# Retention and soft mixture of experts on one core: input rows without gaps, one product moved ahead of a wait, the first expert layer by column halves, one weight load more in flight

## The chip, the cores and the metric

The kernel runs on one core of a Trainium2 chip. The metric is the device time of one execution in microseconds (us), as the median of the runs shown; 0.3% of it is about 0.48 us.

## What is computed

A retention layer (4 batches, 8 heads, 768 steps, head size 64) gives 3072 tokens of 512 values. A soft mixture of 8 experts with 4 slots each follows. All is float32.

```python
state = gamma * state + k_t (outer) v_t          # per batch and head, t = 0..767
y_t   = scale * q_t @ state
x = y as [3072, 512]
logits = x @ phi                                 # phi [512, 32 slots]
d = softmax of logits over the tokens;  slot_input = d.T @ x        # [8 experts, 4, 512]
for e in range(8):
    slot_out[e] = maximum(slot_input[e] @ w1[e], 0) @ w2[e]          # w1 [512, 1024], w2 [1024, 512]
out = (softmax of logits over the slots) @ slot_out                  # [3072, 512]
```

## The kernel before

**Stages.** The sequence is cut into 24 steps of 128 tokens (6 chunks of 4 batches). Two steps make one pass `P` of the loop (12 passes). A pass computes scores (`score_mm`, masked on DVE by `score_mask`), the values under the scores (`attend_mm`), the part from the running state (`carry_mm`, state tile `sall`), the state's update, the turned result (`natural_mm`), and for every four steps the logits and the dispatch of tokens to slots. After the loop comes the dispatch of the last group, whose result is the slot inputs `siT`.

**Experts.** `hidden(g, k)` multiplies slot inputs by first-layer weights. `g` is one of two groups of four experts, `k` one of four pieces of the contraction. All 32 slots are the stationary side; the four experts of a group stand in four column strips of TensorE (`tile_position=(0, 32*j)`), and each of the two halves of the 1024 hidden columns has a PSUM bank of its own. So group 0 ends before group 1 begins, and each group fills two banks. `hidden_t(g)` turns the result, eight 128x128 transposes for each group, and eight small DVE operations for each group take the four slots of each expert out of it (with the ReLU) into `hT`. The second layer runs in three column blocks (`BLOCKS`: 256, 128, 128 wide). `finish` spreads a block to the tokens and stores it; there are eight stores.

**Order.** The order on every engine is the order of the code (`manual_schedule`). All transfers go through one queue, SP's, in the order of the code, and a transfer is issued when its buffer is free and when the transfer eight places before it has landed (eight landing semaphores in turn). Input tiles have 6 buffers (`inp`), weights 13 (`big`), and a ring of 9 half-size tiles (`ring`) serves the rest. Weights are 32 loads of 1 MB: 16 for the first layer, 16 for the second. They are loaded while the loop runs, as many per pass as `PACE` says; in the last pass the freed input buffers and four ring slots take further ones (`load_halves(2)`, `load_weights(2)`), so that 21 loads are issued by then. The other 11 wait until `hidden` has freed a buffer.

**Inputs.** A step's input row holds keys, queries, values and keys again in the other layout, 2048 values for each of 128 partitions. Ten of the 23 rows are loaded without the last quarter (`TURNED` and the last four steps): 1536 of 2048 values, so that 6 KB are read and 2 KB skipped on each partition. The first step has a tensor of its own.

**The beginning** is written out ahead of the loop: score 0, its mask, a turn, the values of heads under score 0 in two parts, with the scores of step 1 between them.

Of the kernel before, what the change touches and what calls it, by code (L numbers as in the profile page):

```python
# [23 lines left out]
NSLOT = 32  # L24
# [19 lines left out]
NRING = 9  # L44
PACE = (1, 1, 1, 2, 1, 2, 1, 2, 2, 0, 2, 2)
TURNED = (0, 1, 2, 3, 4, 8, 12)

K_MASK, K_VSC, K_YT = 0, 128, 176
K_ID, K_QT, K_GC, K_J, K_ALL = 272, 400, 496, 500, 504
# [32 lines left out]
def retention_soft_moe_kernel(  # L82
    ctx: ExitStack,
    tc: tile.TileContext,
    in_: bass.AP,
    phi: bass.AP,
    w1: bass.AP,
    w2: bass.AP,
# [34 lines left out]
    nmc = small("nmc", [128, 2])  # L123
    zrun = zc[:, 0:1]
    wsel = small("wsel", [128, NSLOT])
    siT = small("siT", [128, NK, NSLOT])
# [18 lines left out]


    w1t, w2t, w2n = {}, {}, [0]
    weights = [("w1", 4 * g + 2 * jj, k) for g in range(2) for k in range(NK) for jj in range(2)]
    for cb, (_, w) in enumerate(BLOCKS):
        weights += [("w2", e, cb) for e in range(0, NE, 256 // w)]  # L150

    def load_weights(n):
        for _ in range(n):
            if not weights:
                return
            which, e, k = weights.pop(0)
            t = large(weight_pool[0])
            if which == "w1":
                nc.sync.dma_start(t, w1[e // 2, k])
                w1t[e, k], w1t[e + 1, k] = t[:, 0:FF], t[:, FF:2 * FF]  # L160
            else:
                nc.sync.dma_start(t, w2[w2n[0]])
                w2n[0] += 1
                w = BLOCKS[k][1]
                for j in range(256 // w):
                    for fc in range(NFC):
                        w2t[e + j, k, fc] = t[:, (j * NFC + fc) * w:(j * NFC + fc + 1) * w]

    def load_halves(n):
        for _ in range(n):  # L170
            _, e, k = weights.pop(0)
            assert k == 0
            for h in range(2):
                t = slot()
                nc.sync.dma_start(t, w2[w2n[0], :, h * 1024:(h + 1) * 1024])
                for fc in range(4):
                    w2t[e, k, 4 * h + fc] = t[:, fc * 256:(fc + 1) * 256]
            w2n[0] += 1

    st = {}  # L180
# [2 lines left out]
    def load_in(i):  # L183
        t = large(inp)
        st[i] = dict(kT=t[:, 0:512].rearrange("p (g t) -> p g t", t=C),
                     qT=t[:, 512:1024].rearrange("p (g t) -> p g t", t=C),
                     v=t[:, 1024:1536].rearrange("p (h e) -> p h e", e=D),
                     kn=t[:, 1536:2048].rearrange("p (h d) -> p h d", d=D))
        if i == 0:
            nc.sync.dma_start(t[:, 0:1024], first_[0])  # L190
            nc.sync.dma_start(first, first_[1])
            st[i]["v"] = first[:, K_ALL:K_ALL + 512].rearrange("p (h e) -> p h e", e=D)
        elif i in TURNED or i >= NSTEP - B:
            nc.sync.dma_start(t[:, 0:1536], in_[i - 1, :, 0:1536])
        else:
            nc.sync.dma_start(t, in_[i - 1])

    def turn_k(i, name, ident=ident):
        kp = bank(name)
# [231 lines left out]
    carry_mm(0)  # L431
    turn_k(0, "S", first[:, K_ID:K_ID + 128])
    warm(1)
    attend_mm(0, [0], (0, 1))
    score_mm(1)
    attend_mm(0, [0], (2, 3))
    score_mask(1)
    decay_table(ytab, K_YT)
    turn_k(1, "sm")
    for P in range(NPP):  # L440
# [40 lines left out]
            load_weights(2)  # L481
        attend_mm(P)
        if last:
            break
        attend_copy(P)
        if P < NPP - B // 2:
# [27 lines left out]
            combine_a(g - 1)  # L514

    weight_pool[0] = big
    dispatch_z(g - 1)
    dispatch_acc(g - 1)
    attend_copy(NPP - 1)
# [34 lines left out]
    nc.vector.tensor_scalar(zi, zp, 1e-9, None, ALU.add)  # L554
    nc.vector.reciprocal(zi, zi)
    warm(1, "A0")
    nc.vector.tensor_tensor(siT, sp, zi.unsqueeze(1).broadcast_to([128, NK, NSLOT]), ALU.mult)
    turn_l(g)
    combine_c(g - 1)
    combine_a(g)  # L560

    hs = {}
    hp = {}

    def hidden(g, k):
        if k == 0:
            hp[g] = [bank(n) for n in (("A2", "Y1"), ("Y0", "S"))[g]]
        for hf in range(2):
            for j in range(4):
                nc.tensor.matmul(hp[g][hf][32 * j:32 * j + 32, :], siT[:, k, :],  # L570
                                 w1t[4 * g + j, k][:, hf * 512:(hf + 1) * 512],
                                 start=(k == 0), stop=(k == NK - 1), skip_group_check=True,
                                 tile_position=(0, 32 * j))
        if k == NK - 1:
            hs[g] = slot()
            nc.scalar.copy(hs[g][:, 0:512], hp[g][0])
            nc.vector.tensor_copy(hs[g][:, 512:1024], hp[g][1])

    def hidden_t(g):
        for hf in range(2):  # L580
            tp = bank(("A2", "Y1")[hf]).rearrange("p (f t) -> p f t", t=128)
            for f in range(4):
                fc = hf * 4 + f
                nc.tensor.transpose(tp[:, f, :], hs[g][:, fc * 128:(fc + 1) * 128], ident)
            for j in range(4):
                a = 36 * j + 16 * g
                e = 4 * g + j
                nc.vector.tensor_scalar(hT[hf][:, :, e, 4 * e:4 * e + 4], tp[:, :, a:a + 4], 0.0, None, ALU.max)

    for k in range(NK):  # L590
        hidden(0, k)
        load_weights(2)
        if k == 0:
            hT = [slot().rearrange("p (f e s) -> p f e s", e=NE, s=NSLOT) for _ in range(2)]
            for t in hT:
                nc.vector.memset(t, 0.0)
            combine_b(NGRP - 1)
            combine_c(NGRP - 1)
    hidden(1, 0)
    load_weights(2)  # L600
    hidden(1, 1)
    hidden_t(0)
    load_weights(2)
    hidden(1, 2)
    load_weights(2)
    hidden(1, 3)
    load_weights(len(weights))


    co_tags = ["sm", "A2", "Y1", "A3", "S"]  # L610
    pend = []
# [31 lines left out]

    for cb, (c0, w) in enumerate(BLOCKS):
        op = bank(("A0", "A1")[cb % 2])
        for g in range(2):
            for fc in range(NFC):
                for j in range(4):
                    nc.tensor.matmul(op[32 * j:32 * j + 32, :w], hT[fc // 4][:, fc % 4, 4 * g + j, :],  # L649
                                     w2t[4 * g + j, cb, fc],  # L650
                                     start=(g == 0 and fc == 0), stop=(g == 1 and fc == NFC - 1),
                                     skip_group_check=True, tile_position=(0, 32 * j))
                if cb == 0 and g == 0 and fc == 2:
                    hidden_t(1)
                for f in pend:
                    next(f, None)
# [10 lines left out]
def lay_out(q, k, v, moe_phi, moe_w1, moe_w2):  # L667
    f = np.float32

    def tr(x):  # L670
        x = np.asarray(x).reshape(B, NPAIR, 2, NC, C, D)
        return x.transpose(3, 0, 2, 5, 1, 4).reshape(NSTEP, 128, 512)

    def nat(x):
        x = np.asarray(x).reshape(B, H, NC, C, D)
        return x.transpose(2, 0, 3, 1, 4).reshape(NSTEP, C, 512)


    heads = np.concatenate([head_of(np.arange(2), g) for g in range(NPAIR)])
    phi = np.asarray(moe_phi).reshape(H, D, NSLOT)[heads].reshape(NPAIR, 128, NSLOT).transpose(1, 0, 2)  # L680
    w1 = np.asarray(moe_w1).reshape(NE, H, D, FF)[:, heads].reshape(NE // 2, 2, NK, 128, FF).transpose(0, 2, 3, 1, 4)
    w2 = []
    for c0, w in BLOCKS:
        x = np.asarray(moe_w2)[:, :, c0:c0 + w].reshape(NE * w // 256, 256 // w, NFC, 128, w)
        w2.append(x.transpose(0, 3, 1, 2, 4).reshape(-1, 128, 2 * FF))
    kt, qt, vn = tr(k), tr(q), nat(v)
    return dict(x=np.concatenate([kt, qt, vn, nat(k)], axis=2)[1:], phi=phi,
                w1=w1.reshape(NE // 2, NK, 128, 2 * FF), w2=np.concatenate(w2),
                first=np.stack([np.concatenate([kt[0], qt[0]], axis=1),
                                np.concatenate([constants(), vn[0], np.zeros((128, 1024 - K_ALL - 512), f)], axis=1)]))  # L690

# [20 lines left out]
```

## Time and profile before

| what | value |
|---|---|
| median of 3 runs | 160.35 us (160.19 to 160.71) |
| the profiled execution's own time | 159.53 us |
| its span, first to last instruction | 157.8 us |
| PE busy | 147.1 us (93%) |
| DVE / ACT / POOL busy | 81.5 / 39.8 / 57.7 us |
| data moved by SP's queue | 62.46 MB, 96.8% of 16 engines over the span |

Sums below are made on the profiled execution, which is 0.82 us under the median. A busy share tells how full an engine was, not whether the end waited for it: here PE and the transfer queue are both nearly full, so the rows have to tell which of the two the last store waits for. The transfers of one load are split over 16 transfer engines, and a load has landed when the last of them is done.

### The profile page before, as it was taken

The page shows a single profiled execution, that of the slowest core. Times are in us where ns is not written, and L with a number is a line of the kernel's source. Part 1 is how long each engine was busy: PE and PEld are TensorE (multiplying, and loading weights), DVE is VectorE, ACT ScalarE, POOL GpSimd, SP SyncE. Part 2 cuts the span into 40 slices and gives each one's busy share as a digit, 9 for nine tenths or more (in the row PEclk, how much of TensorE's full clock was granted, in tenths as well). Part 3 has the DMA queues.
Part 4 walks back from the last instruction along what each step waited for, and adds up shares of the span by engine and source line. Part 5 has one row for each costly group of instructions (what it writes and reads, how often), then busy time and mean ns, then how long its engine had stood idle before and what let it go on. Part 6 is the DMA issues. An engine that isn't in the chain of part 4 may idle for free.

```text
span 157.8 us, 5512 instructions
## 1 busy us (share of the span) xinstructions
PE 147.1 (93%) x2418; PEld 108.3 (69%) x2418; DVE 81.5 (52%) x203; ACT 39.8 (25%) x95; POOL 57.7 (37%) x63
## 2 busy tenths in 40 slices
PE   8979999999999999999998989999999999999720
PEld 2569989997999789978996867864324565666400
DVE  0349607573847484758573856578312302555320
ACT  3311551315052305040504031330010100534220
POOL 0343696975737486384738365010100000000000
PEclk9999999999999999999999999999999999999975
DMA  5899999999999999999999999999999999999993
GB/s 205 301 348 422 426 422 415 415 424 413 414 419 418 418 420 420 415 418 420 409 415 423 409 423 415 408 410 397 370 426 422 426 418 424 409 409 416 420 402 125
DMA packets 9816, 62.81 MB, mean 398 GB/s; under 512 B 1088, under 2 KB 1216, under 8 KB 4288
## 3 DMA queue, kind: packets, MB, share of 16 engines
q1 hardware_dynamic: 9792, 62.46, 96.8%
q8 instruction: 19, 0.31, 0.8%
q14 instruction: 5, 0.04, 0.1%
HBM read 56.16 MB, written 6.29 MB: 396 GB/s over the span
## 4 chain that ended last, share of the span: by engine, by line
PE 85%; DMA 4%; DVE 3%; ACT 1%; issue 1%; SPq 1%; ACTq 0%; DVEq 0%
PE A L222 14%; PE Y L255 13%; PE A L649 9%; PE A L299 8%; PE S L283 6%; PE Y L246 6%; DMA b<-in_x_dram 4%; PE Y L570 4%; PE sm L316 4%; PE S L374 3%; PE A L570 2%; PE S L570 2%; PE A L633 2%; DVE r L230 2%; PE A L201 1%; PE sm L633 1%
## 5 line engine op out<-in xcount | busy, mean ns | idle before, releaser
L230 DVE TENSOR_TENSOR r<-A,kt 128x512 f32<-128x512 f32 x46 | 28.7, 682 | 18.3 <-PE A L222 18.3
L207 POOL TENSOR_TENSOR b<-b,qtab 128x512 f32<-128x512 f32 x20 | 25.5, 1280 | 24.0 <-DMA b<-in_x_dram 18.9
L222 PE MATMUL A<-b 64*128 64x128 f32 x384 | 25.2, 279 | 0.9 <-DMA b<-in_x_dram 0.9
L212 POOL TENSOR_TENSOR b<-b,kt 128x512 f32<-128x512 f32 x23 | 23.7, 1049 | 4.7 <-DMA b<-in_x_dram 4.7
L222 PEld LDWEIGHTS A<-b 64*128 64x128 f32 x384 | 22.5, 187 | 4.1 <-issue 2.6
L255 PE MATMUL Y<-r,b 128*64 128x128 f32 x352 | 22.5, 276 | 0.2
L255 PEld LDWEIGHTS Y<-r,b 128*64 128x64 f32 x352 | 19.1, 137 | 2.8 <-issue 2.3
L649 PE MATMUL A<-b,r 128*32 128x128 f32 (+1 forms) x352 | 15.9, 304 | 0.0
L649 PEld LDWEIGHTS A<-b,r 128*32 128x32 f32 x352 | 10.6, 110 | 7.1 <-issue 4.4
L306 ACT COPY r<-A 128x512 f32<-128x512 f32 x23 | 12.4, 591 | 9.9 <-PE A L299 9.9
L299 PE MATMUL A<-kt,r 128*128 128x128 f32 x96 | 13.3, 279 | 0.4 <-ACT r L274 0.4
L299 PEld LDWEIGHTS A<-kt,r 128*128 128x128 f32 x96 | 10.4, 140 | 1.7 <-ACT r L274 0.7
L283 PE MATMUL S<-b 128*64 128x64 f32 x304 | 11.0, 222 | 0.4 <-issue 0.4
L283 PEld LDWEIGHTS S<-b 128*64 128x64 f32 x304 | 10.5, 138 | 0.5 <-issue 0.5
L246 PE MATMUL Y<-b,sst 64*64 64x128 f32 x304 | 10.7, 276 | 0.0
L406 POOL TENSOR_TENSOR cn<-cn,cz 128x128 f32<-128x128 f32 x6 | 2.4, 401 | 19.9 <-DVE cz L405 15.5
L275 DVE COPY r<-Y 128x512 f32<-128x512 f32 x9 | 6.2, 691 | 6.2 <-PE Y L255 6.2
L246 PEld LDWEIGHTS Y<-b,sst 64*64 64x64 f32 x304 | 8.3, 132 | 1.2
L316 PEld LDWEIGHTS sm<-r,phis 128*32 128x32 f32 x192 | 6.2, 110 | 3.3 <-issue 3.3
L633 PE MATMUL A<-cT,r 32*128 32x384 f32 x26 | 8.3, 529 | 0.0
L570 PE MATMUL Y<-b,siT 128*32 128x512 f32 x64 | 8.2, 594 | 0.0
L316 PE MATMUL sm<-r,phis 128*32 128x128 f32 x192 | 7.4, 273 | 0.0
(139 smaller groups left out, 176.4 us busy)
## 6 DMA issues: line engine op xcount, KB each, us to landing
b<-in_w_dram SPq DMA_DIRECT2D x30, 1024.0 KB, 14.8
b<-in_x_dram SPq DMA_DIRECT2D x13, 1024.0 KB, 12.2
b<-in_x_dram SPq DMA_DIRECT2D x10, 768.0 KB, 11.9
out_dram<-b SPq DMA_DIRECT2D x8, 768.0 KB, 8.2
r<-in_w_dram SPq DMA_DIRECT2D x4, 512.0 KB, 11.9
b<-in_first_dram SPq DMA_DIRECT2D x1, 512.0 KB, 3.3
r<-in_first_dram SPq DMA_DIRECT2D x1, 512.0 KB, 4.1
phis<-in_phi_dram SPq DMA_DIRECT2D x1, 64.0 KB, 10.3
```

The source lines that it names most:

```text
L207: nc.gpsimd.tensor_tensor(q, q, qtab, ALU.mult)
L212: nc.gpsimd.tensor_tensor(v, v, vsc[:, i // B, a:b].unsqueeze(2).broadcast_to([128, b - a, D]), ALU.mult)
L222: nc.tensor.matmul(s["sc"][r][:, g, :], s["kT"][half(r), g, :], s["qT"][half(r), g, :], start=True, stop=True, skip_group_check=True)
L230: nc.vector.tensor_tensor(s["A"][:, r, g:g + n], s["sc"][r][:, g:g + n], mask.unsqueeze(1).broadcast_to([128, n, C]), ALU.mult)
L246: nc.tensor.matmul(p["y"][k][b][half(half_of(r, g)), gl, :], sst[(2 * P + k) % B][half(r), g, :], s["qT"][half(r), g, :], start=(gl == 0 a ...
L255: nc.tensor.matmul(pr[P]["y"][k][g // 2][half(half_of(r, g)), g % 2, :], s["v"][:, 2 * g + r, :], s["A"][:, r, g, :], start=(P < B // 2 an ...
L283: nc.tensor.matmul(S_[half(r), k, g, :], s["kn"][:, 2 * g + r, :], s["v"][:, 2 * g + r, :], start=True, stop=True, skip_group_check=True)
L299: nc.tensor.transpose(X[k][:, g * 128:(g + 1) * 128], pr[P]["yT"][:, k, g, :], ident)
L316: nc.tensor.matmul(q["ltp"][32 * j:32 * j + 32, :], phis[:, p, :], st[GRP * g + j]["yT"][:, p, :], start=(p == 0), stop=(p == NPAIR - 1), ...
L570: nc.tensor.matmul(hp[g][hf][32 * j:32 * j + 32, :], siT[:, k, :], w1t[4 * g + j, k][:, hf * 512:(hf + 1) * 512], start=(k == 0), stop=(k ...
L633: nc.tensor.matmul(cp, s4[32 * j:32 * j + 32, m * 128:(m + 1) * 128], cT[32 * j:32 * j + 32, 3 * h:3 * h + 3, :], start=True, stop=True, s ...
L649: nc.tensor.matmul(op[32 * j:32 * j + 32, :w], hT[fc // 4][:, fc % 4, 4 * g + j, :], w2t[4 * g + j, cb, fc], start=(g == 0 and fc == 0), s ...
```

## The change

1. **Rows without gaps.** The ten short rows get a tensor of their own (`in3`, 1536 values per partition, one behind the other), the thirteen whole ones another (`in4`). Size and number of loads stay.
2. **First values.** `attend_mm(0, [0])` does all heads ahead of `score_mm(1)`.
3. **First layer by column halves.** `hidden(hf, g, k)`: both groups of a half accumulate into one bank. For this `siT` is widened (it now lies in `qtab`, which is free by then) and padded with zeros, so that a window of 32 columns that starts 4*j further on holds one expert's slots in rows 0 to 3 (group 0) or 16 to 19 (group 1), and zeros in the other group's rows. One half takes four transposes and two DVE operations. A `w1` load holds one half of four experts, and the order of the `w2` loads of the first block, and of its products, follows the halves.
4. **A 22nd load.** `load_halves(1, sall)` in the last pass loads one more pair of second-layer halves, one into the state tile (no longer read) and one into a ring slot.
5. The zeroing of `hT` goes from DVE to GpSimd (POOL), where the new zeroing of the widened `siT` stands too.

```diff
-            nc.sync.dma_start(t[:, 0:1536], in_[i - 1, :, 0:1536])
+        elif i in LEAN:
+            nc.sync.dma_start(t[:, 0:1536], in3[LEAN.index(i)])
...
-    attend_mm(0, [0], (0, 1))
+    attend_mm(0, [0])
     score_mm(1)
-    attend_mm(0, [0], (2, 3))
...
         attend_mm(P)
         if last:
+            load_halves(1, sall)
             break
...
+    hp = [bank(n) for n in ("A2", "Y0")]
+    hs = slot()
+    def hidden(hf, g, k):
+        for j in range(4):
+            a = g * NK * SIW + k * SIW + 4 * j
+            nc.tensor.matmul(hp[hf][32 * j:32 * j + 32, :], si0[:, a:a + NSLOT],
+                             w1t[hf, g, k][:, j * 512:(j + 1) * 512],
+                             start=(g == 0 and k == 0), stop=(g == 1 and k == NK - 1), skip_group_check=True,
+                             tile_position=(0, 32 * j))
+        if g == 1 and k == NK - 1:
+            h = hs[:, hf * 512:(hf + 1) * 512]
+            nc.scalar.copy(h[:, 0:256], hp[hf][:, 0:256])
+            nc.vector.tensor_copy(h[:, 256:512], hp[hf][:, 256:512])
...
+    for hf in range(2):
+        for g2 in range(2):
+            for k in range(NK):
+                hidden(hf, g2, k)
+                load_weights(1)
...
+                        nc.gpsimd.memset(t, 0.0)
...
+                if (hf, g2, k) == (1, 0, 0):
+                    hidden_t(0)
```

PE at the beginning, before (L222 scores, L255 values under the scores, L201 turn of keys; `A` and `Y` are PSUM banks, `r` and `b` tiles):

```order
L255 MATMUL Y_123<-r 64x128 x4
L222 MATMUL A_137<-b 128x128
L222 MATMUL A_138<-b 128x128
...
L255 MATMUL Y_124<-r 64x128 x4
L201 MATMUL sm<-kt,b 128x128 x4
L222 MATMUL A_169<-b 128x128
```

The same place after (L264 values, L231 scores, L210 turn):

```order
L264 MATMUL Y_122<-r 64x128 x4
L264 MATMUL Y_123<-r 64x128 x4
L231 MATMUL A_140<-b 128x128
L231 MATMUL A_141<-b 128x128
...
L210 MATMUL sm<-kt,b 128x128 x4
L231 MATMUL A_168<-b 128x128
```

The second four products have moved ahead of the eight scores of step 1, which wait for its input.

SP's queue around the last pass, before (`b` and `r` are weight tiles and ring slots):

```order
L159 DMA b<-in_w_dram 128x2048 x3
L162 DMA b<-in_w_dram 128x2048
L175 DMA r<-in_w_dram 128x1024 x4
L162 DMA b<-in_w_dram 128x2048 x13
L639 DMA out_dram<-b 128x1536 x8
```

The same place after (`sst` is the state tile):

```order
L167 DMA b<-in_w_dram 128x2048 x3
L170 DMA b<-in_w_dram 128x2048
L185 DMA r<-in_w_dram 128x1024 x4
L170 DMA b<-in_w_dram 128x2048 x2
L185 DMA sst<-in_w_dram 128x1024
L185 DMA r<-in_w_dram 128x1024
L170 DMA b<-in_w_dram 128x2048 x10
L648 DMA out_dram<-b 128x1536 x8
```

Of the 13 loads before the stores, one has become two halves that stand ahead of the ten which wait for `hidden`.

PE in the first expert layer, the last part before (L570 first layer, L584 transposes, L649 second layer):

```order
L570 MATMUL Y_1756<-b,siT 32x512 x4
L570 MATMUL S<-b,siT 32x512 x4
L584 MATMUL A_1778<-kt,r 128x128 x4
L584 MATMUL Y_1787<-kt,r 128x128 x4
L570 MATMUL Y_1756<-b,siT 32x512 x4
```

The whole layer after, up to the second transposes (L584 first layer, L597 transposes, L659 second layer):

```order
L584 MATMUL A_1696<-b,qtab 32x512 x32
L584 MATMUL Y_1697<-b,qtab 32x512 x4
L597 MATMUL Y_1765<-kt,r 128x128 x4
L584 MATMUL Y_1697<-b,qtab 32x512 x28
...
L597 MATMUL S<-kt,r 128x128 x4
```

The 64 products are the same in number and shape; sixteen transposes have become eight, and one bank is written 32 times in a row.

## Rows read from the trace of the kernel before

**Rows 1.** Page, parts 2 and 3: transfers in 40 slices; instruction fetches (packets, MB, share).

```profile
DMA  5899999999999999999999999999999999999993
GB/s 205 301 348 422 426 422 415 415 424 413 414 419 418 418 420 420 415 418 420 409 415 423 409 423 415 408 410 397 370 426 422 426 418 424 409 409 416 420 402 125
...
q8 instruction: 19, 0.31, 0.8%
```

**Rows 2.** SP's timeline, narrow windows: start and length in us of one issue each.

```profile
150.04 0.33 SPq L639 DMA_DIRECT2D out_dram<-b  x1
151.48 0.33 SPq L639 DMA_DIRECT2D out_dram<-b  x1
...
101.67 0.33 SPq L162 DMA_DIRECT2D b<-in_w_dram  x1
109.81 0.33 SPq L162 DMA_DIRECT2D b<-in_w_dram  x1
```

**Rows 3.** Issues in narrow windows: KB, us to landing (0.8, 150, 151.5, 101.7, 109.8).

```profile
b<-in_first_dram SPq DMA_DIRECT2D x1, 512.0 KB, 3.3
...
out_dram<-b SPq DMA_DIRECT2D x1, 768.0 KB, 4.8
...
out_dram<-b SPq DMA_DIRECT2D x1, 768.0 KB, 5.2
...
b<-in_w_dram SPq DMA_DIRECT2D x1, 1024.0 KB, 12.0
...
b<-in_w_dram SPq DMA_DIRECT2D x1, 1024.0 KB, 6.7
```

**Rows 4.** Stretches: from:to, length, busy of each engine, PEclk, transfer share, GB/s.

```profile
4.00:6.00 2.00, 2.00 (x19) 1.09 (x17) 0.00 (x0) 0.61 (x1) 0.66 (x2) 1.00 0.73 232
8.00:12.00 4.00, 3.20 (x42) 2.67 (x44) 1.97 (x3) 0.59 (x1) 1.88 (x2) 1.00 1.00 347
12.00:13.50 1.50, 1.50 (x35) 1.38 (x32) 1.50 (x3) 0.00 (x0) 0.36 (x2) 1.00 1.03 421
79.50:82.50 3.00, 3.00 (x70) 2.71 (x68) 2.79 (x6) 0.09 (x1) 0.66 (x1) 1.00 1.03 421
109.00:114.00 5.00, 5.00 (x52) 1.53 (x48) 2.51 (x6) 0.12 (x1) 0.40 (x1) 1.00 0.94 357
114.00:120.00 6.00, 6.00 (x60) 2.21 (x56) 1.52 (x9) 0.59 (x1) 0.00 (x0) 1.00 1.01 423
150.00:151.00 1.00, 0.94 (x6) 0.29 (x2) 0.89 (x2) 0.44 (x2) 0.00 (x0) 1.00 0.80 332
```

**Rows 5.** Chain of waits, 5 to 16 us: start, length, what.

```profile
1.64 7.09 DMA b<-in_x_dram
...
8.77 1.16 PE A L222 x16
9.93 0.59 PE Y L255 x8
```

**Rows 6.** Timeline, 6, 11 and 122 us: start, length, engine, line, what, idle before.

```profile
6.23 1.42 DVE L230 TENSOR_TENSOR r<-A,r 128x256 f32<-128x256 f32 x4 [6.23 <-PE A L222]
...
11.13 0.41 PEld L222 LDWEIGHTS A<-b 64*128 64x128 f32 x6 [0.27 <-DMA b<-in_x_dram]
...
121.92 1.04 PE L570 MATMUL S<-b,siT 128*32 128x512 f32 x8
```

**Rows 7.** Chain of waits, 106 to 134 us: first layer, transposes, second layer.

```profile
118.37 0.58 PE A L584 x4
118.96 0.44 PE Y L584 x4
...
122.11 0.86 PE S L570 x8
...
124.26 0.59 PE A L584 x4
...
125.28 5.79 PE A L649 x104
```

More of the change, by code (lines that the diff above doesn't have):

```diff
@@ L46 @@
 TURNED = (0, 1, 2, 3, 4, 8, 12)
+SIW = 48
+LEAN = [i for i in range(1, NSTEP) if i in TURNED or i >= NSTEP - B]
+FULL = [i for i in range(1, NSTEP) if i not in LEAN]
 K_MASK, K_VSC, K_YT = 0, 128, 176
@@ L84, in retention_soft_moe_kernel @@
     tc: tile.TileContext,
-    in_: bass.AP,
+    in3: bass.AP,
+    in4: bass.AP,
     phi: bass.AP,
@@ L147, in retention_soft_moe_kernel, with halves_of @@
     w1t, w2t, w2n = {}, {}, [0]
-    weights = [("w1", 4 * g + 2 * jj, k) for g in range(2) for k in range(NK) for jj in range(2)]
-    for cb, (_, w) in enumerate(BLOCKS):
-        weights += [("w2", e, cb) for e in range(0, NE, 256 // w)]
+    weights = [("w1", hf, g, k) for hf in range(2) for g in range(2) for k in range(NK)]
+    weights += [("w2", 0, e, hf) for hf in range(2) for e in range(0, NE, 2)]
+    weights += [("w2", cb, e, 0) for cb in (1, 2) for e in range(0, NE, 2)]
+    def halves_of(cb, e, hf):
+        if cb == 0:
+            return [[(e + h, 4 * hf + f) for f in range(4)] for h in range(2)]
+        return [[(e + h, fc) for fc in range(NFC)] for h in range(2)]
     def load_weights(n):
@@ L163, in load_weights, with take, load_halves @@
                 w2n[0] += 1
[L164 to L169, printed above, removed]
+                take(at, [t[:, 0:1024], t[:, 1024:2048]])
+    def take(at, tiles):
+        w = BLOCKS[at[0]][1]
+        for t, fcs in zip(tiles, halves_of(*at)):
+            for x, (e, fc) in enumerate(fcs):
+                w2t[e, at[0], fc] = t[:, x * w:(x + 1) * w]
+    def load_halves(n, first_half=None):
         for _ in range(n):
-            _, e, k = weights.pop(0)
-            assert k == 0
+            _, *at = weights.pop(0)
+            tiles = [first_half if first_half is not None else slot(), slot()]
             for h in range(2):
[L174 to L177, printed above, removed]
+                nc.sync.dma_start(tiles[h], w2[w2n[0], :, h * 1024:(h + 1) * 1024])
+            take(at, tiles)
             w2n[0] += 1
@@ L560, in retention_soft_moe_kernel @@
     combine_a(g)
[L562 to L606, printed above, removed]
+    hp = [bank(n) for n in ("A2", "Y0")]
@@ new lines, in hidden_t @@
+    def hidden_t(hf):
+        tp = bank(("Y1", "S")[hf]).rearrange("p (f j t) -> p f j t", j=4, t=32)
+        for f in range(4):
+            fc = hf * 4 + f
+            nc.tensor.transpose(tp[:, f].rearrange("p j t -> p (j t)"), hs[:, fc * 128:(fc + 1) * 128], ident)
+        h = hT[hf].rearrange("p f e s -> p f (e s)")
+        for g in range(2):
+            d = (h[:, :, 0:144].rearrange("p f (j x) -> p f j x", x=36)[:, :, :, 0:4] if g == 0 else
+                 h[:, :, 112:256].rearrange("p f (j x) -> p f j x", x=36)[:, :, :, 32:36])
+            nc.vector.tensor_scalar(d, tp[:, :, :, 16 * g:16 * g + 4], 0.0, None, ALU.max)
@@ new lines, in retention_soft_moe_kernel @@
+    for hf in range(2):
[3 more added lines that the diff above has]
+                load_weights(1)
+                if (hf, g2, k) == (0, 0, 0):
+                    hT = [slot().rearrange("p (f e s) -> p f e s", e=NE, s=NSLOT) for _ in range(2)]
+                    for t in hT:
+                        nc.gpsimd.memset(t, 0.0)
+                    combine_b(NGRP - 1)
+                    combine_c(NGRP - 1)
+                if (hf, g2, k) == (1, 0, 0):
+                    hidden_t(0)
@@ L645, in retention_soft_moe_kernel @@
         op = bank(("A0", "A1")[cb % 2])
[L646 to L656, printed above, removed]
+        units = ([(g, 4 * hf + f) for hf in range(2) for g in range(2) for f in range(4)] if cb == 0 else
+                 [(g, fc) for g in range(2) for fc in range(NFC)])
+        for n, (g, fc) in enumerate(units):
+            for j in range(4):
+                nc.tensor.matmul(op[32 * j:32 * j + 32, :w], hT[fc // 4][:, fc % 4, 4 * g + j, :],
+                                 w2t[4 * g + j, cb, fc], start=(n == 0), stop=(n == len(units) - 1),
+                                 skip_group_check=True, tile_position=(0, 32 * j))
+            if cb == 0 and n == 2:
+                hidden_t(1)
+            for f in pend:
+                next(f, None)
         done = finish(cb, op)
```

37 lines of the change are left out of this document (24 added, 13 removed).

## The prediction

> **What bounds the kernel now.** I read first the busy shares, then the transfers in 40 slices, then the chain of waits, and then the last two stores one by one. The chain puts 85% on PE and PE is busy for 93%, so a reader would take PE for the bound. The transfers say otherwise: from the fourth slice to the 38th the 16 engines are full and move 408 to 426 GB/s, with one dip of some size, at 397 and 370 [rows 1]. Both are full because the queue loads ahead whenever a buffer comes free. The end tells which of the two decides. PE, DVE and ACT are done when the last store is issued, at 151.48 us, and this store lands 5.2 us later, at 156.7; the span ends at 157.8. What would the store take alone? The first load of the kernel finds an empty queue and takes 3.3 us for 512 KB [rows 3]. 256 KB more at 421 GB/s [rows 4] are 0.6 us, so 3.9 us is my estimate for 768 KB. The store therefore stood in the queue for 1.3 us. The store before it is issued at 150.04 and lands at 154.84 [rows 2, 3]; the two land 1.83 us apart, which is 430 GB/s: the transfer engine that finishes last went from one to the other without a pause. So the end is set by the transfer queue, and the last engine's issue could come later by about 1.3 us before the end moves. An earlier issue gives nothing by itself.
>
> One more thing has to be seen. From 150 to 151 us the engines are full for only 0.80 [rows 4], while the store above still waits behind others. So the 16 engines are not equally far: some have run dry while one is behind. Instruction fetches are one cause that the page shows: 19 packets of 16 KB, each on one engine [rows 1]; at a sixteenth of 421 GB/s one takes 0.6 us of that engine's time.
>
> **First values.** Eight values products (0.59 us of PE) stand between the scores of step 1 and the turn of its keys [rows 5]. In the new order they come before the wait for step 1's input, which ends at 8.77 us. They need the masked scores, and DVE is done with these at 6.23 + 1.42 = 7.65 us [rows 6]. The first half runs to 7.9 us, so the second would be done by 8.5: hidden under the wait. But the 0.59 us is not won. The scores of step 2 start at 11.13 us, and what they waited for last is their own input [rows 6]. So PE stands there for 0.59 us instead. Gain: 0 as long as inputs land when they do now. If the cover of the first wait were gone, the cost would be the old 0.59 us, no more.
>
> **Gapless rows.** Bytes, number and order of loads are unchanged, so only the rate can change. The trace of before gives two prices. Steps 1 to 4 all have 2 KB gaps. From 8 to 12 us, where steps 2 and 3 arrive, the engines are full but move 347 GB/s; from 12 to 13.5 us, where the rest of 3 and step 4 arrive with the same gaps, 421; and later rows with gaps, 79.5 to 82.5 us, move 421 as well [rows 4]. If gaps were the cause from 8 to 12, they would have to be harmless elsewhere. Lower bound: 0. Upper bound: 4 us x (421 - 347) / 421 = 0.70 us, and if the poor stretch from 4 to 6 us (232 GB/s) went as well, another 2 x (421 - 232) / 421 = 0.90 us. A loss can't be excluded, since no row shows 6 KB rows laid end to end; by the same two rates it is bounded by 0.7 us at the start, where the engines already run at the poor rate, so I take up to 0.3. I take 0, because the nearest rows, the same loads with the same gaps, run at full rate twice.
> The Trainium skill (DMA: Bandwidth & Descriptors, Specifications) gives 512 B as the smallest transfer for line rate. By that rule a 6 KB run is as good with a gap behind it as without, and this term is 0; by the row of 8 to 12 us alone it would be 0.7. The rule does not explain that row, so I don't let it close the case.
>
> **Column halves.** 64 products of 512 columns stay 64, at 0.86 us for four [rows 7]. Before, the first call of `hidden_t` costs 0.58 + 0.44 us on PE, and the second begins in the same way; now each has four transposes instead of eight. Taking the cheaper half, PE loses 2 x 0.44 = 0.9 us of work. The copies that the transposes wait for are halves on ACT and DVE, and they run beside four products (0.86 us) the first time and beside three units of the second layer (a unit is 5.79 / 13 = 0.45 us) the second time [rows 7], so they cost nothing; without that cover each would cost some 0.5 us. The 16 small DVE operations become 4, and the zeroing moves to POOL, which is idle there: no one waits. All of this lies on PE's path: stores are issued about 0.9 us earlier. By the first part above this shortens nothing, since each store then waits 0.9 us longer in the queue.
>
> **The 22nd load.** From 109 to 114 us the queue runs low, because the eleven remaining loads wait until the first layer has freed buffers: the first is issued at 109.81 [rows 2]. The mean rate there is 357 against 423 GB/s after it [rows 4], which is 5 x (423 - 357) / 423 = 0.78 us of all engines. The change puts 1 MB more (2.5 us of transfer) in the queue before that, and a call of the new `hidden` frees a buffer after 0.86 us instead of 1.72. The dip is gone. The new halves wait for landings of the loads eight places before. The second waits for one that stands 4 MB ahead of the load that lands at 113.7 us (next paragraph), so it lands at about 113.7 - 4 x 2.5 = 103.7; the loads behind it on SP wait for the first layer, which begins after that, and lose nothing.
> What is the dip worth at the end? Of the two loads on either side of it, one is issued at 101.67 and lands after 12.0 us, at 113.7, the next at 109.81 and lands after 6.7, at 116.5 [rows 2, 3]. They land 2.8 us apart. 1 MB at 423 GB/s takes 2.5. So the engine that finishes last lost 0.3 us in the dip, while the mean engine lost 0.78: the engines that ran dry were those ahead. I take 0.3, and 0 and 0.78 as ends (0 because a fetch on that one engine would cost it more than the whole 0.3).
> The Trainium skill (DMA: Bandwidth & Descriptors, iDMA fabric) notes that a bulk load "runs at the pace of its slowest engine". By that the dip counts 0.3; by the mean share it would count 0.78. The landing rows agree with the sentence.
>
> **The sum.** Profiled execution: 159.53 us (span 157.8 and 1.7 around it). First values 0, gapless rows 0, column halves 0 at the end (0.9 on PE), 22nd load -0.3: 159.2. The median of the runs is 0.82 us above this execution; I take the difference to it: 160.35 - 0.3 = **160.05 us**. What is late next is the same thing as now, the last engine's queue, with about 1.3 + 0.9 us of slack for PE.
>
> **Rivals.**
> *The gaps did cost at the start.* Then the whole stream of transfers moves 0.7 us earlier, PE with it (the scores of step 2 no longer wait, and the 0.59 us of the first values comes free), and with the dip it is 160.35 - 0.7 - 0.3 = 159.35 us; with the stretch from 4 to 6 us too, 158.45. For it: rows 4 from 8 to 12 us. Against: the same rows at 12 and at 79.5 us.
> *The queue behaves as one pipe.* If lagging engines even out, the full 0.78 us comes off, and PE, 0.9 earlier, lets it: 159.55 us. For it: the 0.80 share before the last store. Against: the landings at the dip.
> *One bank is slower.* Four products after four now add into the same bank, where before two banks took turns. Four take 1.04 us from the first start to the last end [rows 6] but begin every 0.86; if each four had to wait for the end of the ones before, that is 16 x 0.18 = 2.9 us more. Less the 0.9 saved, PE would be 2.0 us later; 1.3 us of that is slack of the last store, and the end is 0.7 us later: 161.05. It decides once PE is later by more than 1.3 us. Against it: the second layer adds 13 units into one bank at 0.45 us for 256 columns, just half of 0.86 for 512 [rows 7].
> *The edits don't act.* The first values are such a case already; if the two halves were issued only after `hidden` began, the dip would stay: 160.35.
>
> **How the numbers follow.** A measurement of this kernel can tell 0.3%, 0.48 us, from no change. Forecast (0 to 0.6 us off, and a spread of runs of 0.3 either way): 0.55, of which 0.10 is faster by over 0.3%, 0.40 within, 0.05 slower. Gaps: 0.27, faster. One pipe: 0.08, faster. One bank, or rows that load worse end to end: 0.10, slower. So faster 0.45, within 0.3% 0.40, slower 0.15. The range goes from 158.9, which leaves out the far end of the gaps' case, to 160.8, which takes in runs above the median and a part of the bank's case.
>
> **What would show it.** Right: the slices at 109 to 114 us at 415 or more; a chain in which the transposes stand as x4 once per half; the last store issued about 0.9 us earlier than 151.48 and landing more than 5.2 us after its issue. 8 to 12 us still near 347 GB/s would settle the gaps against the rival; 400 or more there would make the forecast wrong, as would a last store that lands 3.9 us after its issue (then PE sets the end) or products of the first layer at more than 0.9 us for four.

## The result, and the profile after

| what | before | after |
|---|---|---|
| median of the runs made side by side | 160.53 us (160.04 to 161.45) | 158.97 us (158.51 to 159.44) |
| ratio | | 0.9886, interval 0.9848 to 0.9925 |
| the profiled execution's own time | 159.53 us | 159.04 us |
| its span | 157.8 us | 157.3 us |
| PE busy | 147.1 us (93%) | 146.4 us (93%) |

The change is faster by 1.1%, about 1.6 us; 160.05 was forecast. The profiled execution of before is 1.0 us under its median here, that of after 0.1 over its own. So the two traces show a third of the gain. Below, sizes are taken from the runs and places from the traces.

The page of after, transfers in 40 slices:

```profile
DMA  5999999999999999999999999999999999999974
GB/s 172 400 402 429 423 413 420 417 423 415 413 416 417 421 417 421 415 417 417 409 421 415 417 406 413 405 382 424 401 421 425 423 419 421 415 413 401 388 298 192
```

Against [rows 1], the second and third slices are at 400 and 402 where 301 and 348 stood; the dip in slices 28 and 29 (397 and 370) is nearly gone, with 382 left in slice 27; and there is a new hole near the end, 298 where 402 stood. The same stretches as in [rows 4] (from:to, length, busy of each engine, PEclk, transfer share, GB/s):

```profile
4.00:6.00 2.00, 1.83 (x21) 1.26 (x20) 0.24 (x1) 0.31 (x1) 0.27 (x1) 1.00 1.01 388
8.00:12.00 4.00, 3.37 (x46) 2.89 (x48) 2.22 (x4) 0.59 (x1) 2.08 (x2) 1.00 1.02 407
109.00:114.00 5.00, 5.00 (x49) 1.54 (x52) 1.72 (x8) 0.31 (x1) 0.40 (x1) 1.00 1.01 401
114.00:120.00 6.00, 6.00 (x56) 1.86 (x52) 0.78 (x3) 0.37 (x1) 0.00 (x0) 1.00 1.02 425
150.00:151.00 1.00, 1.00 (x6) 0.51 (x4) 0.59 (x2) 0.01 (x1) 0.00 (x0) 0.59 0.35 139
```

From 8 to 12 us 407 instead of 347: the rival's mark. From 4 to 6 us 388 instead of 232, but other kernels show below that this stretch does not follow the rows. From 109 to 114 us 401 instead of 357. In the last row the clock falls and the transfers are at 0.35: they wait for PE. The last two stores in SP's timeline of after (start and length in us of the issue), then in its list of issues, each in a narrow window (KB, us from issue to landing):

```profile
150.19 0.33 SPq L648 DMA_DIRECT2D out_dram<-b  x1
...
152.37 0.33 SPq L648 DMA_DIRECT2D out_dram<-b  x1
```

```profile
out_dram<-b SPq DMA_DIRECT2D x1, 768.0 KB, 4.3
...
out_dram<-b SPq DMA_DIRECT2D x1, 768.0 KB, 3.9
```

The last store is issued 0.9 us later than before [rows 2], not earlier, and lands 3.9 us after its issue, which is what the prediction had estimated for a store that finds the queue empty. The chain of waits at the beginning and through the first layer (start, length, what):

```profile
2.11 8.23 DMA b<-in_x_dram
...
10.38 1.16 PE A L231 x16
...
50.73 0.55 issue
...
83.69 0.55 issue
...
91.29 0.39 issue
...
109.04 6.99 PE A L584 x64
116.03 0.86 PE Y L584 x8
116.88 0.59 PE Y L597 x4
...
124.91 0.59 PE S L597 x4
```

PE has the scores of step 2 at 10.38 instead of 11.13 [rows 6], 0.75 us ahead, but begins the first layer at 109.04, 1.0 us behind before, whose chain has

```profile
58.47 0.12 issue
...
83.98 0.43 issue
...
108.00 0.93 PE A L570 x8
```

Two things took the lead. Three pauses stand in the chain of after as "issue", 1.49 us in all, where before has 0.55 between 20 and 100 us (pauses under 0.1 us left out); the profile names nothing that they wait for. And DVE was held up. Its timeline in before, in after, and POOL's in after (start, length, what):

```profile
103.80 0.23 DVE L527 TENSOR_SCALAR nj<-kt,nmc 128x4 f32<-128x4 f32 x1
```

```profile
103.91 1.23 DVE L541 TENSOR_SCALAR nj<-kt,nmc 128x4 f32<-128x4 f32 x1
104.05 1.09 DVE L315 COPY r<-A 128x512 f32<-128x512 f32 x1
```

```profile
103.27 1.84 POOL L612 MEMSET r<- 128x1024 f32 x2
```

The operation that took 0.23 us takes 1.23, and PE waits for what it makes. It begins while POOL zeroes `hT` and ends at 105.14; POOL is done at 105.11. Not every DVE operation was held: two on 128x1 results that began under the same fills, at 103.33 and 103.66, took 0.29 and 0.21 us, as in before.

### The profile page after: what moved, and what is told of

Same layout as the page of the kernel before. It is cut to its first block, busy times and chain, and to the rows that moved or that the text cites. A ratio compares the mean times of both kernels' runs of the same rounds, so it can differ in the third digit from the quotient of the medians.

```text
span 157.3 us, 5480 instructions
## 1 busy us (share of the span) xinstructions
PE 146.4 (93%) x2410; PEld 107.6 (68%) x2410; DVE 78.3 (50%) x189; ACT 39.5 (25%) x95; POOL 59.7 (38%) x66
## 4 chain that ended last, share of the span: by engine, by line
PE 86%; DMA 5%; DVE 2%; issue 1%; SPq 1%; ACT 0%
PE A L231 14%; PE Y L264 14%; PE A L659 9%; PE A L308 7%; PE Y L255 6%; PE S L292 6%; DMA b<-in_x_dram 5%; PE Y L584 4%; PE A L584 4%; PE sm L325 4%; PE S L383 3%; PE A L642 2%; PE S L642 2%; PE A L210 1%; PE sm L642 1%
## 5 line engine op out<-in xcount | busy, mean ns | idle before, releaser
L231 PE MATMUL A<-b 64*128 64x128 f32 x384 | 25.2, 279 | 0.8 <-DMA b<-in_x_dram 0.6
L231 PEld LDWEIGHTS A<-b 64*128 64x128 f32 x384 | 22.6, 187 | 3.7 <-issue 1.8
L264 PE MATMUL Y<-r,b 128*64 128x128 f32 x352 | 22.4, 276 | 0.4 <-issue 0.4
L264 PEld LDWEIGHTS Y<-r,b 128*64 128x64 f32 x352 | 19.1, 137 | 2.8 <-issue 2.2
L659 PE MATMUL A<-b,r 128*32 128x128 f32 (+1 forms) x336 | 15.9, 300 | 0.0
L659 PEld LDWEIGHTS A<-b,r 128*32 128x32 f32 x336 | 10.3, 110 | 6.4 <-issue 4.4
L292 PEld LDWEIGHTS S<-b 128*64 128x64 f32 x304 | 10.6, 138 | 1.3 <-issue 1.3
L255 PE MATMUL Y<-b,sst 64*64 64x128 f32 x304 | 10.6, 276 | 0.0
L255 PEld LDWEIGHTS Y<-b,sst 64*64 64x64 f32 x304 | 8.2, 132 | 1.2
L642 PE MATMUL A<-cT,r 32*128 32x384 f32 x26 | 9.0, 559 | 0.0
L301 DVE TENSOR_TENSOR sst<-sst,S 128x256 f32<-128x256 f32 x16 | 6.0, 418 | 3.3 <-PE S L292 3.3
```

Of the source, the lines that this page charges most:

```text
L231: nc.tensor.matmul(s["sc"][r][:, g, :], s["kT"][half(r), g, :], s["qT"][half(r), g, :], start=True, stop=True, skip_group_check=True)
L255: nc.tensor.matmul(p["y"][k][b][half(half_of(r, g)), gl, :], sst[(2 * P + k) % B][half(r), g, :], s["qT"][half(r), g, :], start=(gl == 0 a ...
L292: nc.tensor.matmul(S_[half(r), k, g, :], s["kn"][:, 2 * g + r, :], s["v"][:, 2 * g + r, :], start=True, stop=True, skip_group_check=True)
L642: nc.tensor.matmul(cp, s4[32 * j:32 * j + 32, m * 128:(m + 1) * 128], cT[32 * j:32 * j + 32, 3 * h:3 * h + 3, :], start=True, stop=True, s ...
```

## The experiments

Each kernel's ratio is to runs of the kernel before on the same chip.

**Each part alone, and taken out.** `e1_gapless_alone` is before with the gapless rows:

```diff
-            nc.sync.dma_start(t[:, 0:1536], in_[i - 1, :, 0:1536])
+            nc.sync.dma_start(t[:, 0:1536], in3[LEAN.index(i)])
```

> The kernel before with one edit: the ten short input rows lie end to end in a tensor of their own. Theory (the gaps slowed the first rows): 8 to 12 us moves 400 GB/s or more instead of 347, the stream of transfers runs about 1.0 us earlier from 13 us on, and the kernel is 0.7 to 1.2 us faster than before, because the last store waits in that stream. Rival (the recorded forecast, gaps cost nothing): 8 to 12 us stays near 350 GB/s, time within 0.3 us of before. Second rival (PE sets the end): the stream is earlier but the last store is issued no earlier and the time moves by less than 0.4 us.

`e2_after_gapped` is after with that line put back:

> The changed kernel with the old input rows (gaps of 2 KB); all other edits stay. Theory: 8 to 12 us falls back to about 350 GB/s and the kernel loses 0.7 to 1.2 us against the changed one, so that it stands within 0.5 us of the kernel before. Rival (the gain of 1.5 us came mostly from the 22nd load and the column halves): it stays 0.8 us or more faster than before.

`e4_22nd_alone` is before with the 22nd load:

```diff
         attend_mm(P)
         if last:
+            load_halves(1, sall)
             break
```

> The kernel before with one edit: one more second-layer load in the last pass, half into the state tile and half into a ring slot. Theory (the dip hits only the engines that are ahead): the dip at 109 to 114 us goes (415 GB/s or more), and the time moves by 0 to 0.4 us. Rival (the queue behaves as one pipe): the time falls by 0.6 us or more.

`e5_gapless_22nd` is before with both, so without the column halves and the new order of the first values:

> The kernel before with two edits: gapless rows and the 22nd load; the first expert layer and the first values as before. Theory (the stream gains 1 us or more at the start, but loses it again where the queue runs low at 109 to 114 us, as the run with gapless rows alone shows with 315 GB/s there; the 22nd load fills that hole): the dip is at 390 GB/s or more, and the time is 1.0 to 1.6 us under the kernel before, close to the changed kernel, though each edit alone gave 0.5 and 0.3 us. Rival (PE's 0.9 us in the first expert layer is what was missing): 0.3 to 0.8 us under the kernel before.

`e6_after_no_22nd` is after without that line:

> The changed kernel without its 22nd load; gapless rows, column halves and first values stay. Theory (a hole in the queue gives the start's gain back): 109 to 114 us falls to about 340 GB/s and the time is 0.5 to 1.1 us above the changed kernel. Rival (the first layer by halves, which frees a buffer after 0.86 us instead of 1.72, closes the hole by itself): the time stays within 0.3 us of the changed kernel.

| kernel | gapless | 22nd load | halves, first values | median us | ratio, interval | GB/s 8 to 12 | GB/s 109 to 114 |
|---|---|---|---|---|---|---|---|
| before | | | | 160.5 | 1 | 347 | 357 |
| e1 | yes | | | 159.92 | 0.9968 (0.9936 to 0.9999) | 419 | 315 |
| e4 | | yes | | 160.08 | 0.9985 (0.9956 to 1.0014) | 338 | 399 |
| e5 | yes | yes | | 158.90 | 0.9889 (0.9852 to 0.9926) | 413 | 392 |
| e2 | | yes | yes | 160.29 | 0.9985 (0.995 to 1.0019) | 351 | 413 |
| e6 | yes | | yes | 159.96 | 0.995 (0.9919 to 0.9981) | 399 | 275 |
| after | yes | yes | yes | 158.97 | 0.9886 (0.9848 to 0.9925) | 407 | 401 |

Some expectations were missed: e1 gained 0.5 us and not 0.7 to 1.2, the hole is filled to 399 and not 415 in e4, and it is deeper in e6 (275) than the 340 expected.

Two readings. The whole gain is there without the column halves and the first values (e5 and after are level). And rows and load need each other: the rows alone give 0.3%, the load alone 0.15%, both 1.1%; taken out of the whole change, the load costs 0.6% and the rows 1.0%. e8 and e9 below are two more kernels in which only the rows are changed; they gain 0.6% and 0.5%, so by the ratios the two edits together are worth 0.4% to 0.6% more than their sum. The stretch at 109 to 114 us shows a part of the reason, in e1, then e6, then e5:

```profile
109.00:114.00 5.00, 5.00 (x52) 1.56 (x48) 2.43 (x6) 0.05 (x1) 0.40 (x1) 1.00 0.85 315
```

```profile
109.00:114.00 5.00, 5.00 (x47) 1.52 (x50) 2.12 (x9) 0.31 (x1) 0.40 (x1) 1.00 0.79 275
```

```profile
109.00:114.00 5.00, 5.00 (x52) 1.56 (x48) 2.45 (x6) 0.06 (x1) 0.40 (x1) 1.00 1.02 392
```

When the stream of transfers starts earlier, it reaches the place where the queue has nothing more to load earlier too, while the first layer, which frees the buffers, begins no earlier. So the hole grows. Against the rate from 114 to 120 us of the same kernel it is worth 0.78 us in before, 5 x (430 - 315) / 430 = 1.3 us in e1, 5 x (415 - 275) / 415 = 1.7 us in e6, and 0.4 us with the load (e5, against 425). This is the mean of the 16 engines, and the intervals above, about 0.5 us either way, leave the size of the interplay rough.

The end waits for the engine that finishes last, and for it the landings of the loads on either side of the hole tell. In e1 they are issued at 101.60 and 109.74, in e6 at 102.33 and 110.62 (KB, us from issue to landing; e1, then e6):

```profile
b<-in_w_dram SPq DMA_DIRECT2D x1, 1024.0 KB, 10.8
...
b<-in_w_dram SPq DMA_DIRECT2D x1, 1024.0 KB, 5.7
```

```profile
b<-in_w_dram SPq DMA_DIRECT2D x1, 1024.0 KB, 10.1
...
b<-in_w_dram SPq DMA_DIRECT2D x1, 1024.0 KB, 5.9
```

They land 3.0 us apart in e1 and 4.1 in e6, against 2.8 in before, and 1 MB takes 2.5. So the last engine lost 0.3 us in the hole in before, 0.5 in e1 and 1.6 in e6. In e6 this covers its distance from after at the last store (157.4 against 156.2). In e1 it does not: its lead on before is 1.3 us ahead of the hole and still 1.0 behind it, and is lost later. And e8 has as deep a hole as e1, but its last store lands at 156.0, no later than that of after (e8's hole; its last store in SP's timeline and in the list of issues):

```profile
109.00:114.00 5.00, 5.00 (x54) 1.44 (x45) 2.17 (x6) 0.13 (x1) 0.40 (x1) 1.00 0.84 321
```

```profile
151.15 0.33 SPq L642 DMA_DIRECT2D out_dram<-b  x1
```

```profile
out_dram<-b SPq DMA_DIRECT2D x1, 768.0 KB, 4.8
```

So a trace shows the hole taking the lead back in e6; that it does so in e1 and e8 is not shown. The times fit that: executions of e1, e6 and e8 range from 158.75 to 161.15 us, those of after and e5 from 158.51 to 159.44. Kernels with the rows alone come close to the full gain in some executions and miss it in others.

**Which property of the rows costs.** `e7_own_tensor_gap`: the short rows in a tensor of their own, still 2048 values apart. `e8_small_gap`: 1600 apart. `e9_far_rows`: 2112 apart, so with a longer gap than before. `e10_whole_rows`: the old tensor, with steps 1 to 4 loaded whole.

```diff
-    return dict(x3=x[LEAN][:, :, 0:1536], x4=x[FULL], phi=phi,
+    return dict(x3=x[LEAN][:, :, 0:2048], x4=x[FULL], phi=phi,      # e7; 1600 in e8, 2112 (rows padded) in e9
...
-        elif i in TURNED or i >= NSTEP - B:
+        elif i >= NSTEP - B or i in (8, 12):                        # e10
```

> The kernel before with the ten short rows in a tensor of their own, but 2048 values apart as before, so that the gap of 2 KB stays. Theory (it is the gap between the rows): 8 to 12 us stays at 335 to 360 GB/s as in the kernel before. Rival (it is the place of the rows in memory, a tensor of their own): 400 GB/s or more, as with gapless rows.

> The kernel before with the ten short rows in a tensor of their own, 1600 values apart, so that each row of 6 KB has a gap of 256 bytes behind it. If any gap slows the first rows, 8 to 12 us moves 335 to 360 GB/s; if the distance of 8 KB from row to row does it, 400 GB/s or more.

> The kernel before, with the ten short rows in a tensor of their own whose rows stand 2112 values (8448 bytes) apart: 6144 bytes read, 2304 skipped, so the gap is larger than before (2048 bytes) and the distance is no longer 8192. If it is the distance of just 8192 bytes between partitions that cost at the start, 8 to 12 us goes to 400 GB/s or more and the time is near that of the rows with a small gap (159.2, alone about 1 us under before). If a long skip behind each run is what costs, 8 to 12 us stays at 330 to 355 GB/s and the time is within 0.4 us of before (160.5).

> The kernel before, with the rows of steps 1 to 4 loaded whole (8192 bytes read at a distance of 8192, nothing skipped; 1.05 MB more in all, of which the last quarter is overwritten by the turned keys as before). If the skip is what costs, the rate from 8 to 12 us is 400 GB/s or more. If the start costs whatever the rows are like (the distance alone, or the state of the chip at that time), it is near 350 there. Step 4's input lands 2.5 us of transfer later than before (15.3) less what the rate gives back: near 16.8 in the first case, near 17.8 in the second. The time is 160.5 plus up to 2 us, less what the queue's hole at 109 to 114 us lets the late stream make up; the rate and not the time is the verdict.

8 to 12 us in e7, e8, e9 and e10, in this order:

```profile
8.00:12.00 4.00, 3.74 (x52) 2.86 (x48) 2.28 (x3) 0.59 (x1) 2.09 (x2) 1.00 0.97 350
```

```profile
8.00:12.00 4.00, 4.00 (x58) 3.25 (x54) 2.26 (x4) 0.59 (x1) 2.33 (x3) 1.00 1.02 417
```

```profile
8.00:12.00 4.00, 4.00 (x58) 3.42 (x60) 2.88 (x5) 0.58 (x1) 2.34 (x3) 1.00 1.01 411
```

```profile
8.00:12.00 4.00, 2.76 (x34) 2.23 (x36) 1.62 (x3) 0.51 (x1) 1.44 (x2) 1.00 1.00 424
```

Between 8 and 12 us the tensor's place is not it (350). A gap as such is not it: 256 bytes and even 2304 bytes skipped run at 417 and 411. Whole rows at a distance of 8192 bytes run at 424. What is slow is 6144 bytes read at a distance of just 8192. The times go with it: e7 160.77 us (ratio 1.0002, 0.9973 to 1.0031), e8 159.19 (0.9942, 0.9901 to 0.9982), e9 159.76 (0.9952, 0.9913 to 0.999), and e10, with 1.05 MB more to load, 161.88 (1.0094, 1.0058 to 1.013). So e1, e8 and e9 are three kernels in which the rows alone gain 0.3 to 0.6%. One mark of e10 came out the other way: its step 4 landed at 18.0 us (issued at 3.69, 14.3 later), near the 17.8 expected if the rate stayed poor. But steps 1 to 3 landed at 9.0, 11.5 and 14.1, 2.5 us apart, as 1 MB takes at full rate; what made step 4 land 3.9 us behind step 3 is not shown.

The stretch from 4 to 6 us does not follow the rows. Here it is in e4 (6144 bytes at 8192, as in before), e11 (gapless) and e10 (whole rows):

```profile
4.00:6.00 2.00, 2.00 (x17) 1.00 (x17) 0.00 (x0) 0.60 (x1) 0.55 (x1) 1.00 0.89 337
```

```profile
4.00:6.00 2.00, 2.00 (x13) 1.00 (x13) 0.00 (x0) 0.29 (x1) 0.24 (x1) 1.00 0.88 353
```

```profile
4.00:6.00 2.00, 2.00 (x22) 1.38 (x21) 0.22 (x1) 0.61 (x1) 0.76 (x2) 1.00 0.78 301
```

With the rows of before, e4, e7 and e2 are at 337, 326 and 360 there. So the 232 of before is not the price of its rows; the stretch from 8 to 12 us separates the kernels, this one does not.

**The later rows.** `e12_first_four_22nd` is e5 with gapless rows for steps 1 to 4 only:

```diff
-LEAN = [i for i in range(1, NSTEP) if i in TURNED or i >= NSTEP - B]
+LEAN = [i for i in range(1, NSTEP) if i in TURNED and i <= 4]
```

> The kernel before with the 22nd load, and with gapless rows for steps 1 to 4 only; the six later short rows (steps 8, 12 and the last four) keep their 6 KB at a distance of 8 KB. With all ten rows gapless it was 158.90 us, with none 160.08. If only the first loads of the kernel suffer from the distance, as the row of 421 GB/s at 79.5 to 82.5 us says, this kernel is at 158.9 plus or minus 0.4, with 8 to 12 us at 400 GB/s or more. If the later rows cost as well (six rows, 768 KB each, at 347 instead of 421 GB/s would be 2.0 us on the transfers, of which a part could hide), it is 159.6 or more.

159.22 us, ratio 0.9914 (0.988 to 0.9947). 0.3 us above e5, which the intervals don't tell apart, and below 159.6. Two of the six later rows, still 8192 bytes apart, arrive from 79.5 to 82.5 us, and at full rate:

```profile
79.50:82.50 3.00, 3.00 (x69) 2.71 (x68) 2.72 (x6) 0.00 (x0) 0.90 (x1) 1.00 1.04 429
```

**Who sets the end.** `e3_after_dve_zero` is after with the zeroing of `hT` back on DVE; `e11_dve_zero_clock` adds three empty products in PE's pauses at 146 and 147 us:

```diff
-                        nc.gpsimd.memset(t, 0.0)
+                        nc.vector.memset(t, 0.0)                    # e3 and e11
...
         nc.vector.tensor_copy(os_[:, :w], op[:, :w])
+        if cb == 2:
+            warm(1, "A1", 128)                                      # e11 alone
...
         nc.vector.tensor_copy(s4[:, :w], rp[:, :w])
+        if cb == 2:
+            warm(2, "A1", 128)
```

> The changed kernel with the two zeroing instructions of hT back on DVE, at the same place in the code. Theory (GpSimd's zeroing, 103.27 to 105.11 us in the changed kernel's trace, held DVE up): the small DVE product nj takes 0.23 us again instead of 1.23 and the copy behind it 0.69 instead of 1.09, the first expert layer begins 1.0 us earlier relative to the last pass, and the last store is issued 1.0 us earlier. The time falls by 0.3 to 1.0 us if PE sets the end now, by less than 0.3 us if the transfer engine that is last does. Rival (the long nj had another cause): nj stays over 1 us.

> The changed kernel with the zeroing of hT on DVE, and three empty products of 128 columns in the last block's two pauses of PE (0.41 and 0.47 us at 146 and 147 us), into a bank that is free. In the kernel without them the granted clock falls to half at 149 us, seven of the last products take 0.82 us instead of 0.48, the last store is issued at 151.47 and lands 4.70 us later. If PE with this clock sets the end, the clock stays at 1.00 to 151 us, the last store is issued at 150.5 to 150.9, and the time is 158.2 to 158.6. If the transfers alone set the end (my theory for the kernel before), the store lands at 155.7 or later all the same and the time stays within 0.3 us of 158.9.

e3 is at 158.92 us (0.9899, 0.9865 to 0.9933), e11 at 159.2 (0.9908, 0.9874 to 0.9942). The last store in e3, in SP's timeline and in the list of issues:

```profile
151.47 0.33 SPq L648 DMA_DIRECT2D out_dram<-b  x1
```

```profile
out_dram<-b SPq DMA_DIRECT2D x1, 768.0 KB, 4.7
```

The same in e11:

```profile
149.87 0.33 SPq L652 DMA_DIRECT2D out_dram<-b  x1
```

```profile
out_dram<-b SPq DMA_DIRECT2D x1, 768.0 KB, 6.1
```

One of PE's last products in its timeline, in after and then in e11:

```profile
150.15 0.81 PE L642 MATMUL S<-cT,r 32*128 32x384 f32 x1
```

```profile
148.39 0.48 PE L646 MATMUL S<-cT,r 32*128 32x384 f32 x1
```

In e3 the small operation on DVE is back at 0.23 us, and the store is issued 0.9 us earlier than in after. In e11 PE also keeps its clock (0.48 us for a product that takes 0.81 at the half clock of after), and the store is issued at 149.87, 2.5 us earlier than in after. It lands at 156.2, 156.2 and 156.0. PE can be 2.5 us earlier and the end doesn't move: the transfers set it. e11 was meant to beat the change and does not.

Where the 2.5 us come from is seen at the first layer, in the chain of e3 and then of e11:

```profile
108.14 6.99 PE A L584 x64
```

```profile
57.70 0.12 issue
...
83.39 0.28 issue
...
107.26 6.99 PE A L584 x64
```

With the zeroing on DVE the layer begins 0.9 us earlier than in after. e11's code is that of e3 up to the last block, but its pauses come to 0.40 us where e3 has the 1.49 of after, and it begins another 0.9 us earlier, 0.74 ahead of before. So the changed kernel does not always have these pauses. The rest, 0.7 us, goes with the clock. That the empty products kept it is not shown: before has the same pauses without them, and one of its last products still runs at full clock (PE's timeline):

```profile
147.00 0.49 PE L622 MATMUL Y<-os,rep 128*128 128x128 f32 x2 [0.41 <-DVE os L618]
148.04 0.56 PE L633 MATMUL S<-cT,r 32*128 32x384 f32 x1 [0.54 <-DVE r L623]
...
149.99 0.48 PE L633 MATMUL S<-cT,r 32*128 32x384 f32 x1
```

## Why the prediction was wrong, and where it was right

**What bounds the kernel: right.** The prediction had the last store wait 1.3 us in the queue, so that PE has slack and gains nothing by being earlier. e11 shows it most plainly, 2.5 us for nothing. The estimate of 3.9 us for a store that finds the queue empty was measured in after, 3.9. Its own mark against itself, a store landing 3.9 us after its issue, did come true, but only because PE was late enough to use the slack up: with PE 0.9 us earlier in e3 the landing is only 0.1 us earlier.

**Gapless rows: the step that failed.** Taken as 0, with ends of 0 and 1.6 us (0.70 and 0.90). The rows are worth 0.5 to 0.9 us alone (e1, e8, e9, by the ratios) and 1.2 to 1.6 beside the 22nd load (e4 to e5 and e2 to after, by medians and by ratios). Step 4's load lands 1.0 us earlier in after and 1.8 us earlier in e1 (issued at 3.67, 3.78 and 3.83 us in before, after and e1, and landed 11.7, 10.6 and 9.7 us later); before is late here for its kind, since e2, e4 and e7, with the same rows, land it at 15.0 and not 15.3. The reason given for 0 was that the same loads with the same gaps run at 421 GB/s at 12 and at 79.5 us. These rows were read rightly (e12: 429), but what they say holds for their place alone. The stretch that the change touches, 8 to 12 us, had a row of its own, 347, and no other explanation for it. So the rival "the gaps did cost at the start" came true in its mechanism, for this stretch: it gave 159.35. Its lower figure, 158.45, took in the stretch from 4 to 6 us, which does not go with the rows (e4, e11, e10); that 158.97 lies between the two is no support for it. Nor does it speak for the forecast that 158.97 lies within the stated range, since the range was stretched to take in most of this rival. The Trainium skill was cited with a rule by which the term is 0 (DMA: Bandwidth & Descriptors, Specifications: 512 B as the smallest transfer for line rate), and the measured 347 at runs of 6 KB says that this rule is not enough. A row of the same page of the Trainium skill, one that the prediction did not weigh, is nearer (section Latency and other measured facts, HBM row pitch at large powers of two): copies whose partitions lie 512 KiB or more apart are slow, and padding the distance by 4 KiB gives the rate back. Here the distance is 8 KiB, the padding that suffices 256 bytes (e9), and whole rows at 8 KiB are not slow (e10); so it is at most a relative of that rule.

**The 22nd load: right in place, wrong in being counted by itself.** The hole at 109 to 114 us was there and the load fills most of it: 401, though 415 was asked for. Alone it gives 0.24 us by the ratio of e4, the 0.3 of the prediction within what the runs can tell; the rival of one pipe, 0.78, lies just outside that interval. But the two edits were added as if independent. Once the stream starts earlier the same hole is larger, and the load is worth about 1.0 us (159.92 to 158.90, and 159.96 to 158.97). How much of this the hole itself costs is shown in e6 alone.

**First values: right.** They had 0 as long as inputs land when they do. Inputs landed earlier, but e5, which leaves this order as it was, is as fast.

**Column halves: right at the end, wrong on the way.** 0 at the end holds (e5). The transposes stand as x4 once per half, and four products (x8 in the chain, two records for each) start 0.86 us after the four before, so the rival "one bank is slower" falls. But in after the 0.9 us earlier store did not come: "POOL, which is idle there: no one waits" was the wrong sentence. The zeroing held DVE for 1.0 us and so PE. With it back on DVE (e3) the store is still issued when before's is, at 151.47, since PE's clock fell in the last block. In e11, where neither stands in the way, the layer begins 0.74 us ahead of before and the store is issued 1.6 us ahead, so the 0.9 us are won in between, as forecast. That all this costs or gives nothing at the end (e3, e11) is the slack again, not the step.
The Trainium skill (SBUF — State Buffer, SBUF: two separate sides) describes the port pair that DVE and GpSimd share as "an **exclusive lock**, not a bandwidth split": whichever instruction that needs the pair starts first holds it to its end. The trace agrees: the 0.23 us operation lasts until POOL's two fills end. An idle engine was checked; whom it locks out was not.

**What stays open.** Why 6 KB at a distance of 8 KB is slow from 8 to 12 us and at full rate later: no run separates the time from what else is in flight. In e1's trace the stream is 1.3 us ahead of before at the load ahead of the hole, and its last store lands when before's does; by the landings the hole accounts for 0.3 us of that, and which engine lost the rest, and to what, is not shown. Nor is what PE's "issue" pauses wait for, nor on what the fall of its clock in after and e3 depends.

## What to carry to other kernels

Where a stretch runs below the rate of its neighbours, the row of that stretch is the price; rows of the same operation elsewhere don't clear it. When a change starts a full queue earlier, look for the next place where the queue runs empty for want of buffers: without more to load there the lead can be given back, and an edit that fills that hole may be worth more than it was alone. The price of such a hole is read from the landings on its two sides, not from the mean rate. Before work is moved to an idle engine, ask which other engine it locks out while it runs.

## What the runs showed of the hardware that was not expected

- 6144 bytes per partition read at a distance of 8192 bytes run at 338 to 351 GB/s from 8 to 12 us (before, e2, e4, e7); at distances of 6144, 6400 and 8448 bytes at 399 to 419; whole rows of 8192 bytes at 424; and 6144 at 8192 from 79.5 to 82.5 us at 417 to 429 (before, e2, e4, e7, e12).
- Two fills of 128x1024 on POOL (1.84 us) stretched a DVE operation on 128x4 values from 0.23 to 1.23 us; two with 128x1 results under the same fills kept their 0.29 and 0.21 us.
- PE pauses for which the trace shows no releaser came to 1.49 us between 20 and 100 us in after and e3, 0.55 in before and 0.40 in e11. With 1.49 (and the zeroing in after) PE's start, 0.7 to 0.8 us earlier, did not last to the first layer; in e11 it did.
- In after and e3 PE's clock fell to half, the lower of its two levels, in the last block (0.59 as the mean from 150 to 151 us in after, 0.50 in e3), behind pauses of PE (in e3 0.41 and 0.47 us at 146 and 147 us). In e11, with empty products in the pauses, its last products took 0.48 us, but so did those of before, with pauses of 0.41 and 0.54 us. It made no difference to the end.
